# Loading the second table of the taps' transform behind the taps, four small edits early in the token stage, and later first one-hot bursts

## The chip, the cores and the metric

The kernel runs on one core of one Trainium2 chip. The metric is the device time of one execution in microseconds (us). Five engines work side by side, each through its own instructions in order: TensorE (PE in the profile; its weight loads are PEld), VectorE (DVE), ScalarE (ACT), GpSimd (POOL) and SyncE (SP), whose queue issues nearly all DMA transfers. They meet only at semaphores: an instruction whose input is not there yet holds up everything behind it on its own engine.

## The reference, cut to what matters

```python
x = A_u                                              # 2048 tokens x 576 channels
g = sigmoid((x * gate_w).sum(-1, keepdims=True))
# a: a long convolution along the tokens, each channel with its own 2048 taps
K = einsum("dn,dnl,dn->dl", C, exp(dt * A * l), dt * B).real
a = irfft(rfft(x, 4096) * rfft(K, 4096))[:2048] + x * Dskip
# b: experts chosen by product keys, 32 heads, 4096 experts
q = einsum("nd,dhc->nhc", x, w_q)
s1, s2 = q[..., :128] @ k1.T, q[..., 128:] @ k2.T    # 64 scores each; the best 2 of each
cand = the 4 sums of the best; the 2 largest go through a softmax -> gate, expert index
b = sum over heads and choices of gate * gelu(x . u[index]) * v[index]
out = g * a + (1 - g) * b
```

## The kernel before, in words

All matrix work runs on TensorE, most of it as three half-precision products per wanted product (a value is split into a high and a low f16 part: high x high, high x low, low x high). The stages, with the names that the profile shows for the tiles that TensorE writes:

- Start: the first 512 tokens (tile xs, its last 64 channels xr) and the first 512 experts' input rows (us, ur) are loaded in pieces; ScalarE squares each piece, small matmuls with a matrix of ones add the squares up (tile sq), VectorE makes power-of-two scales from the sum (`root_scale`), and both are split into f16 parts (xb and uhl; the part above 512 rows of the weights is wrem). For the first tokens six matmuls into a bank named x run ahead with results that nobody reads.
- Token stage: every token with every expert (tile a: 8 expert blocks of 512, 4 token blocks of 512, 4 matmul groups each) and the scores of the keys (tile s: 8 x 16 groups). A group is 14 matmuls of 512 columns. VectorE takes the best of the scores (MAX8, FIND_INDEX8); the results of a go as `go` to a buffer in memory, g_d. Between these groups stand 16 steps of the first Fourier stage of the tokens (`u_stage1`, tile u), the generation of the taps (phases kP, products on GpSimd and VectorE, then matmuls into tile kb, stored to k_d), and the folding of the keys into the query weights (wb).
- `freq()` starts when the last taps are on their way to k_d. It loads the tables of the taps' transform (tk, two of 1 MB) and the taps (ksb, four loads of 128 partitions x 9216 bytes from k_d), runs `k_stage1` (32 steps, tile k, step w reads table w // 16), then the frequency products (pr, pi, pv). `v_norm`, started by it, adds up the squares of the experts' output rows v; its one matmul (pvn) gives their scale, and only then `v_work` splits the eight tables vhl: table c is loaded into the place of table c + 1, the last one into a slot called vs; ScalarE writes each high part, VectorE the low part with SCALAR_TENSOR_TENSOR, two rows of blocks (a pair of instructions) at a time, two pairs per table.
- Last stage, one of 16 token tiles after the other in the order 0, 15, 1, 14, 2, ...: `prep(t)` loads g_d back (gl), applies the gelu on ScalarE, builds one-hot tiles A and Bg on VectorE (`onehot`, four sets, q = 0 to 3), multiplies them on TensorE into tile S (two sets to a burst, bursts named S1_0/S1_1 and S1_2/S1_3 for token tile 1), multiplies gl by S on VectorE, and splits the product into wh. Then 192 matmuls of 288 columns per token tile (tile o) multiply wh by the tables vhl in the order of the experts: 24 matmuls per table. `y_part` (tile y) adds the convolution's result.

The order of the instructions is set when the program is built. Generators yield to one another; each engine has a running estimate of when it will be free (class `Engine`, `dma`, `mm`), `ready` and `need` hold a piece of work until its inputs and its PSUM banks are estimated to be there, and `late` adds to that estimate. Whoever is ready first is written first, so a small change of one estimate can change the order of everything behind it. Nothing is decided at run time: what the estimate has wrong becomes a wait.

All matmuls come from the helper on line 214, all vector and scalar instructions from line 134, all DMA issues from line 205.

Of the kernel before, what the change touches and what calls it, by code (L numbers as in the profile page):

```python
# [18 lines left out]
OP = mybir.AluOpType  # L19
# [119 lines left out]
def body(ctx: ExitStack, tc: tile.TileContext, xT, au, par, logdt, dskip, gatew, wq, kT, uT, vv,  # L139
# [305 lines left out]
    def squares(a, r, sq, dst):  # L445

        acc = newcol(), newcol()
        S.activation(sq[:, 0:4, :], a, AF.Square, accum_out=sc[:, acc[0]])
        S.activation(sq[:, 4, :], r, AF.Square, accum_out=sc[:, acc[1]])
        yield from ready(sq)  # L450
        tag = side()
        yield from need(tag)
        p = bank(tag, "sq")
        mm(p[:, 0:2], onesb, short(acc[0].start, 2), True, True, 0.05)
        yield from ready(p)
        V.tensor_reduce(out=dst, in_=p[:, 0:2], axis=AX, op=OP.add)
        free(tag, dst)

    marks = {"x": [], "s": [], "h": [], "u": []}
    first_u = [None, None]  # L460
    ahead, normed = [], []

    def x_norm(tb, sq):

        yield from need("kb")
        p = bank("kb", f"x{tb}")
# [36 lines left out]
    def scale_first(a, r, sq, keep=None):  # L503
# [13 lines left out]
        p = bank("kb", "sq")  # L517
        for n, c in enumerate(acc):
            mm(p[:, 0:1], onesb, short(c.start, 1), n == 0, n == len(PARTS), 0.05)
# [554 lines left out]
    def u_stage1():  # L1074
# [32 lines left out]
        for p in range(NT):  # L1107
# [18 lines left out]
            for hh in range(2):  # L1126
                cs = slice(288 * hh, 288 * hh + 288)
                for n, (z, w) in enumerate(((0, 0), (0, 1), (1, 0))):
                    for g in range(2):
                        r = slice(64 * g, 64 * g + 64)  # L1130
                        mm(pbs[hh][g][:, :288], tu[r, z], h[r, w, cs], n == 0, n == 2, 0.063)
# [144 lines left out]
    def freq():  # L1276
# [7 lines left out]
        for w0, tkt in zip((0, 16), tabs):  # L1284
            dma(tkt, tk_d[:, w0:w0 + 16, :])
        for j in range(4):
            while wire[0] > clock[0] + 2:
                yield 0.3
            dma(ksb[:, j].rearrange("p c w i -> p c (w i)"),
                k_d[:, 32 * j:32 * j + 32].rearrange("c l z m n -> (l z m) c n"))  # L1290
        spawn(v_norm(), 12)
# [28 lines left out]
    def u_load(c):  # L1320
# [3 lines left out]
        if c:  # L1324
            dma(a, uT[0:512, cs].rearrange("(k p) n -> p k n", p=128))
        dma(r[0:64], uT[512:576, cs])
        if c:
            dma(r[64:128], uT[512:576, cs])
        else:
# [5 lines left out]
    def u_build(c):  # L1335
# [24 lines left out]
        if c == 0:  # L1360
            for k in range(4):
                S.activation(hl[:, 0, k, :], a[:, k, :], AF.Copy, scale=s)
# [147 lines left out]
    def prep(t):  # L1510
# [19 lines left out]
        for q in (0, 2):  # L1530
            yield from ready(*oh[q], *oh[q + 1], late=2.5 if t in ORDER[:3] else 0.0)
# [335 lines left out]
```

## Time and profile before

| what | value |
|---|---|
| median of 3 runs (lowest, highest) | 1441.61 us (1441.29, 1444.52) |
| profiled execution, its own time | 1442.26 us |
| span from the first to the last instruction in it | 1440.3 us |
| TensorE busy | 1421.2 us, 99% of the span |
| VectorE busy | 1161.8 us, 81% |
| ScalarE / GpSimd busy | 769.9 us / 484.2 us |
| granted TensorE clock | 1.000 |

The span leaves 19.1 us in which TensorE does nothing. An engine's idle time is given with what ended it: `[0.58 <-DMA ksb<-k_d]` means 0.58 us of idle time before this row, ended by the landing of that transfer. A timeline row is start, duration, engine, line, operation, out<-in, and xN where N like instructions were merged; the next start tells more than the duration, since matmuls and vector instructions overlap their ends.

### The profile page before, as it was taken

The numbers are of one execution on the slowest core, as the hardware profiler recorded it, in microseconds if no ns is written. First come the engines' busy times: TensorE is split into PE (matmuls) and PEld (weight loads), VectorE is DVE, ScalarE is ACT, GpSimd is POOL, SyncE is SP. The second block draws the span as 40 slices with busy tenths as digits, with TensorE's granted clock in tenths as the row PEclk, the third lists the DMA queues.
The fourth block names the chain that finished last, engine by engine and source line by source line (L and its number), as shares of the span: only waits on it lengthen the run. The fifth ranks groups of instructions, "written<-read, shape, count | busy, mean of one in ns | idle before, by whom it ended". The sixth has DMA issues, their size and how long they took to land.

```text
span 1440.3 us, 40769 instructions
## 1 busy us (share of the span) xinstructions
PE 1421.2 (99%) x16151; PEld 835.6 (58%) x16153; DVE 1161.8 (81%) x4595; ACT 769.9 (53%) x1281; POOL 484.2 (34%) x492
## 2 busy tenths in 40 slices
PE   7999999999999999999999999999999999999999
PEld 3444445455455445455555444456787787787785
DVE  6899899879886997875999897689877777877840
ACT  6346876796784876844655655666333223323310
POOL 0325357547356346230547899700000000000000
PEclk9999999999999999999999999999999999999999
DMA  8235323442334323159675677967443332442400
GB/s 302 75 116 165 90 74 121 126 144 72 109 100 154 93 93 115 49 172 308 222 264 191 243 258 271 307 216 249 151 131 130 117 122 95 136 147 69 159 10 17
DMA packets 134239, 215.43 MB, mean 150 GB/s; under 512 B 11040, under 2 KB 79904, under 8 KB 127648
## 3 DMA queue, kind: packets, MB, share of 16 engines
q1 hardware_dynamic: 133952, 212.80, 45.2%
q8 instruction: 127, 2.08, 0.6%
q14 instruction: 64, 0.52, 0.1%
q10 hardware_dynamic: 96, 0.02, 0.0%
HBM read 141.48 MB, written 71.30 MB: 148 GB/s over the span
## 4 chain that ended last, share of the span: by engine, by line
PE 87%; DVE 5%; DMA 1%; issue 0%; ACT 0%; SPq 0%; DVEq 0%
PE o L214 25%; PE s L214 24%; PE a L214 21%; PE S L214 3%; PE kb L214 2%; PE pr L214 2%; PE wb L214 2%; PE pv L214 1%; PE y L214 1%; PE kP L214 1%; PE k L214 1%; PE u L214 1%; DVE vhl L134 1%; DMA wq<-in_wq_dram 1%; DVE gl L134 1%; DVE A L134 1%
## 5 line engine op out<-in xcount | busy, mean ns | idle before, releaser
L214 PE MATMUL o<-vhl,wh 128*128 128x288 f16 (+2 forms) x3072 | 382.7, 286 | 0.0
L214 PE MATMUL s<-whl,xb 128*128 128x512 f16 x1536 | 363.9, 379 | 0.0
L214 PE MATMUL a<-xb,uhl 128*128 128x512 f16 x1536 | 358.8, 379 | 0.5 <-ACT uhl L134 0.3
L214 PEld LDWEIGHTS <-wh 128*128 128x128 f16 x3072 | 292.4, 98 | 84.1 <-issue 3.7
L214 PEld LDWEIGHTS <-xb 128*128 128x128 f16 x1792 | 170.7, 98 | 209.2 <-issue 14.5
L214 PEld LDWEIGHTS <-uhl 128*128 128x128 f16 x1536 | 147.3, 98 | 177.4 <-issue 3.2
L134 DVE FIND_INDEX8 i<-m,s 128x8 uint32<-128x64 f32 x1024 | 206.1, 219 | 0.0
L134 ACT ACTIVATE wh<-gl,s_wg 128x1024 f16<-128x1024 f32 x64 | 69.0, 1137 | 197.5 <-DVE gl L134 197.5
L134 DVE MAX8 m<-s 128x8 f32<-128x64 f32 x1024 | 145.9, 212 | 30.4 <-PE s L214 29.4
L134 POOL TENSOR_TENSOR CS<-CS,ex 128x512 f32<-128x512 f32 x72 | 98.0, 1392 | 147.5 <-DVE ex L134 146.1
L134 DVE TENSOR_TENSOR gl<-S,gl 128x256 f32<-128x256 f32 x256 | 88.4, 413 | 36.8 <-PE S L214 36.8
L134 ACT ACTIVATE go<-a,i_a 128x512 f32<-128x512 f32 x93 | 62.5, 684 | 97.2 <-PE a L214 70.2
L134 POOL TENSOR_TENSOR e<-aN,rt 128x512 f32<-128x512 f32 x72 | 83.2, 1176 | 49.9 <-PE kb L214 43.8
L134 DVE TENSOR_TENSOR A<-iota_a,vals 128x2048 f16<-128x2048 f16 x64 | 77.9, 1217 | 23.3 <-PE S L214 23.3
L134 ACT ACTIVATE gl<-gl 128x1024 f32<-128x1024 f32 x64 | 63.6, 1045 | 45.3 <-DMA gl<-g_d 36.8
L134 DVE SCALAR_TENSOR_TENSOR wh<-gl,s_wg,wh 128x1024 f16<-128x1024 f32 x62 | 77.6, 1279 | 12.4 <-ACT wh L134 12.3
L214 PE MATMUL s<-wrem,xb 128*128 128x512 f16 x256 | 76.2, 379 | 0.0
L214 PE MATMUL a<-xb,wrem 128*128 128x512 f16 x256 | 75.9, 379 | 0.0
L134 DVE MATCH_VALUE_LOAD i<-m,s 128x8 f32 x1024 | 69.4, 68 | 0.1
L134 ACT ACTIVATE CS<-CS 128x1024 f32<-128x1024 f32 x57 | 59.2, 1044 | 7.3 <-DVE CS L134 7.3
L134 POOL TENSOR_TENSOR ex<-ex,gN 128x512 f32<-128x512 f32 x36 | 44.8, 1256 | 53.3 <-ACT ex L134 53.1
L134 DVE SCALAR_TENSOR_TENSOR ya<-o,om,ya 128x288 f32<-128x288 f32 (+2 forms) x32 | 15.1, 512 | 55.4 <-PE o L214 55.4
(209 smaller groups left out, 2098.3 us busy)
## 6 DMA issues: line engine op xcount, KB each, us to landing
g_d<-go SPq DMA_DIRECT2D x128, 256.0 KB, 2.5
gl<-g_d SPq DMA_DIRECT2D x32, 1024.0 KB, 5.5
wq<-in_wq_dram SPq DMA_DIRECT2D x16, 1152.0 KB, 5.6
su_d<-us SPq DMA_DIRECT2D x32, 288.0 KB, 2.6
sk_d<-k1o SPq DMA_DIRECT2D x32, 288.0 KB, 2.7
ui<-su_d SPq DMA_DIRECT2D x16, 576.0 KB, 3.9
ki<-sk_d SPq DMA_DIRECT2D x16, 576.0 KB, 5.5
vn<-in_vv_dram SPq DMA_DIRECT2D x32, 288.0 KB, 5.4
```

The source lines that it names most:

```text
L134: return f(*a, **k)
L214: T.matmul(o, l, r, start=start, stop=stop)
```

## The change

Seven places of the source change. In `squares` the small square (the last channels) is now written ahead of the large one, and in `u_load` the small loads ahead of the large one for the expert blocks after the first. The bank x0 is taken early and nine more matmuls with unread results are spread over the two sums of squares at the start (`scale_first`). The first block of 512 columns of uhl is split between ScalarE and VectorE. In `u_stage1` the low table's product is moved ahead of the product with the low part of the input, so that this low part (tile uh, written last) is read by the last four of twelve matmuls and not by the third to sixth of a half. The second tk table is issued behind the four loads of the taps. The first three token tiles' one-hot bursts get 3.8 instead of 2.5 added to their estimate.

```diff
--- before.py
+++ after.py
@@ -445,8 +445,8 @@
     def squares(a, r, sq, dst):
 
         acc = newcol(), newcol()
+        S.activation(sq[:, 4, :], r, AF.Square, accum_out=sc[:, acc[1]])
         S.activation(sq[:, 0:4, :], a, AF.Square, accum_out=sc[:, acc[0]])
-        S.activation(sq[:, 4, :], r, AF.Square, accum_out=sc[:, acc[1]])
         yield from ready(sq)
         tag = side()
         yield from need(tag)
@@ -458,12 +458,14 @@
 
     marks = {"x": [], "s": [], "h": [], "u": []}
     first_u = [None, None]
+    first_x = []
     ahead, normed = [], []
 
     def x_norm(tb, sq):
 
-        yield from need("kb")
-        p = bank("kb", f"x{tb}")
+        if tb:
+            yield from need("kb")
+        p = bank("kb", f"x{tb}") if tb else first_x[1]
         if tb == 0:
             for k in range(6):
                 mm(p, onesb, sq[:, k % 4, :], True, True)
@@ -515,7 +517,14 @@
         yield from ready(sq)
         yield from need("kb")
         p = bank("kb", "sq")
+        if keep is None:
+            yield from need("kb")
+            first_x.extend((sq, bank("kb", "x0")))
+        idle_on, over = first_x
+        idle_at = ((), (4,) * 4, (0,), (2,)) if keep is None else ((), (), (0, 1), (2,))
         for n, c in enumerate(acc):
+            for k in idle_at[n]:
+                mm(over, onesb, idle_on[:, k], True, True)
             mm(p[:, 0:1], onesb, short(c.start, 1), n == 0, n == len(PARTS), 0.05)
         yield from ready(p)
         out = root_scale(p[:, 0:1], 1.02)
@@ -1123,9 +1132,9 @@
             yield from need(tag, 4)
             hungry[0] = False
             pbs = [[bank(tag, f"u1_{p}_{g}_{hh}") for g in range(2)] for hh in range(2)]
-            for hh in range(2):
-                cs = slice(288 * hh, 288 * hh + 288)
-                for n, (z, w) in enumerate(((0, 0), (0, 1), (1, 0))):
+            for n, (z, w) in enumerate(((0, 0), (1, 0), (0, 1))):
+                for hh in range(2):
+                    cs = slice(288 * hh, 288 * hh + 288)
                     for g in range(2):
                         r = slice(64 * g, 64 * g + 64)
                         mm(pbs[hh][g][:, :288], tu[r, z], h[r, w, cs], n == 0, n == 2, 0.063)
@@ -1281,13 +1290,13 @@
         ksb = KS.__enter__().tile([128, 4, NCK // 2, 32, 2 * NI], F16, name="ksb")
         fk = FK.__enter__()
         tabs = [fk.tile([128, 16, 2, 128], F16, tag="tk", name=f"tk{w0}", bufs=2) for w0 in (0, 16)]
-        for w0, tkt in zip((0, 16), tabs):
-            dma(tkt, tk_d[:, w0:w0 + 16, :])
+        dma(tabs[0], tk_d[:, 0:16, :])
         for j in range(4):
             while wire[0] > clock[0] + 2:
                 yield 0.3
             dma(ksb[:, j].rearrange("p c w i -> p c (w i)"),
                 k_d[:, 32 * j:32 * j + 32].rearrange("c l z m n -> (l z m) c n"))
+        dma(tabs[1], tk_d[:, 16:32, :])
         spawn(v_norm(), 12)
         spawn(gating(0), 20)
         yield from k_stage1(ksb, fk, tabs)
@@ -1321,11 +1330,10 @@
         a = slot([4, 512], F32, f"us{c}")
         r = actp.tile([128, 512], F32, tag="ur", name=f"ur{c}")
         cs = slice(512 * c, 512 * c + 512)
-        if c:
-            dma(a, uT[0:512, cs].rearrange("(k p) n -> p k n", p=128))
         dma(r[0:64], uT[512:576, cs])
         if c:
             dma(r[64:128], uT[512:576, cs])
+            dma(a, uT[0:512, cs].rearrange("(k p) n -> p k n", p=128))
         else:
             halves_load(a, uT, cs)
         return a, r
@@ -1359,7 +1367,10 @@
         rem = wrems[c % 2]
         if c == 0:
             for k in range(4):
-                S.activation(hl[:, 0, k, :], a[:, k, :], AF.Copy, scale=s)
+                w = 512 if k else 256
+                S.activation(hl[:, 0, k, :w], a[:, k, :w], AF.Copy, scale=s)
+                if k == 0:
+                    V.tensor_scalar(hl[:, 0, k, w:], a[:, k, w:], s, None, op0=OP.mult)
                 marks["h"].append(S.free + 0.28)
             S.activation(rem[:, 0, :], r, AF.Copy, scale=s)
             marks["h"].append(S.free + 0.28)
@@ -1528,7 +1539,7 @@
                 yield 0.3
             oh = {q: onehot(t, q) for q in range(3)}
         for q in (0, 2):
-            yield from ready(*oh[q], *oh[q + 1], late=2.5 if t in ORDER[:3] else 0.0)
+            yield from ready(*oh[q], *oh[q + 1], late=3.8 if t in ORDER[:3] else 0.0)
             yield from need("wb", 4)
             pbs = []
             for d in (q, q + 1):
```

Up to the 25th step of the phases (near 465 us of the trace before) TensorE's order is the same but for the nine added matmuls and the exchange in u. From there on the order differs until the third pair of token tiles of the last stage, and is the same again to the end. Three places of it follow. Names end in the buffer's number, which differs between the two programs.

SyncE's queue where the transform's tables (tk0, tk16) and the taps (ksb) are loaded, before:

```order
L205 DMA wq5_0_8158<-in_wq_dram 128x2304
L205 DMA tk0_8173<-in_tk_dram 128x4096
L205 DMA tk16_8174<-in_tk_dram 128x4096
L205 DMA ksb_8169<-k_d_68 128x18x256
L205 DMA g_d_65<-go6_0_1_8295 128x4x128
L205 DMA ksb_8169<-k_d_68 128x18x256
L205 DMA wq5_1_8348<-in_wq_dram 128x2304
L205 DMA g_d_65<-go6_0_2_8359 128x4x128
L205 DMA g_d_65<-go6_0_3_8385 128x4x128
L205 DMA ksb_8169<-k_d_68 128x18x256
L205 DMA g_d_65<-go6_1_0_8405 128x4x128
L205 DMA ksb_8169<-k_d_68 128x18x256
```

and now:

```order
L205 DMA wq5_0_8056<-in_wq_dram 128x2304
L205 DMA k_d_68<-ko_8207 128x1024
L205 DMA tk0_8267<-in_tk_dram 128x4096
L205 DMA ksb_8263<-k_d_68 128x18x256
L205 DMA wq5_1_8315<-in_wq_dram 128x2304
L205 DMA ksb_8263<-k_d_68 128x18x256 x3
L205 DMA tk16_8268<-in_tk_dram 128x4096
L205 DMA g_d_65<-go6_1_1_8433 128x4x128
```

The loads of the taps stand closer together with one load of query weights (wq) between them, and the second table behind them. On TensorE, counted in the order, 170 matmuls of 512 columns stood between the last taps' products (kb34) and the first step of k before; 104 stand there now, and the two foldings wb5 in both.

SyncE's queue at the last two loads of the v tables, vhl7 (raw rows of table 6) and vs (of table 7), before:

```order
L205 DMA vhl7_12507<-in_vv_dram 128x4x576
L205 DMA g_d_65<-go7_1_0_13173 128x4x128
L205 DMA g_d_65<-go7_1_1_13201 128x4x128
L205 DMA g_d_65<-go7_1_2_13220 128x4x128
L205 DMA vs_13408<-in_vv_dram 128x4x576
L205 DMA g_d_65<-go7_1_3_13418 128x4x128
L205 DMA g_d_65<-go7_2_0_13423 128x4x128
L205 DMA g_d_65<-go7_2_1_13436 128x4x128
L205 DMA g_d_65<-go7_2_2_13591 128x4x128
L205 DMA gl1_0_13616<-g_d_65 128x2048
L205 DMA gl1_1_13617<-g_d_65 128x2048
```

and now:

```order
L205 DMA vhl7_12509<-in_vv_dram 128x4x576
L205 DMA gl1_0_13608<-g_d_65 128x2048
L205 DMA gl1_1_13609<-g_d_65 128x2048
L205 DMA g_d_65<-go7_2_3_13633 128x4x128
L205 DMA db_13658<-in_dskip_dram 128x576
L205 DMA tf0_13663<-in_tf_dram 128x256
L205 DMA yz0_13662<-z_d_69 128x1x576 x4
L205 DMA ya0_13660<-in_au_dram 32x576 x4
L205 DMA ya15_13661<-in_au_dram 32x576 x4
L205 DMA vs_13890<-in_vv_dram 128x4x576
```

The load of vs stood ahead of gl1, the gelu input of token tile 1; it now stands behind gl1 and behind the inputs of y. The matmul pvn, from which the v tables' scale comes, stood 316 matmuls of a ahead of the first o before and stands 266 ahead of it now.

VectorE's queue after the last one-hot set of token tile 1 (Bg1_3), before, where the last pair for table 7 comes behind four products with S:

```order
L134 TENSOR_TENSOR Bg1_3_13865<-Be1_3_13863,vals_80 128x512 x2
L134 TENSOR_TENSOR gl1_0_13616<-S1_0_0_13729,gl1_0_13616 128x16x16
L134 TENSOR_TENSOR gl1_1_13617<-S1_0_0_13729,gl1_1_13617 128x16x16
L134 TENSOR_TENSOR gl1_0_13616<-S1_0_1_13730,gl1_0_13616 128x16x16
L134 TENSOR_TENSOR gl1_1_13617<-S1_0_1_13730,gl1_1_13617 128x16x16
L134 SCALAR_TENSOR_TENSOR vhl7_12507<-vs_13408,sci_76,vhl7_12507 128x576 x2
L134 TENSOR_TENSOR gl1_0_13616<-S1_1_0_13795,gl1_0_13616 128x16x16
```

and now, some twenty rows further on, from the last products of S1_3 to the second pair for table 7:

```order
L134 TENSOR_TENSOR gl1_1_13609<-S1_3_0_14024,gl1_1_13609 128x16x16
L134 TENSOR_TENSOR gl1_0_13608<-S1_3_1_14025,gl1_0_13608 128x16x16
L134 TENSOR_TENSOR gl1_1_13609<-S1_3_1_14025,gl1_1_13609 128x16x16
L134 SCALAR_TENSOR_TENSOR ya0_13660<-y0_0_0_14143,iuk_94,ya0_13660 128x288
L134 SCALAR_TENSOR_TENSOR ya0_13660<-y0_0_1_14148,iuk_94,ya0_13660 128x288
L134 SCALAR_TENSOR_TENSOR wh1_1_14109<-gl1_0_13608,s_wg_92,wh1_0_14108 128x1024
L134 SCALAR_TENSOR_TENSOR vhl7_12509<-vs_13890,sci_76,vhl7_12509 128x576 x2
L134 SCALAR_TENSOR_TENSOR ya15_13661<-y0_1_0_14153,iuk_94,ya15_13661 128x288
L134 SCALAR_TENSOR_TENSOR ya15_13661<-y0_1_1_14158,iuk_94,ya15_13661 128x288
L134 SCALAR_TENSOR_TENSOR wh1_1_14109<-gl1_0_13608,s_wg_92,wh1_0_14108 128x1024
L134 SCALAR_TENSOR_TENSOR vhl7_12509<-vs_13890,sci_76,vhl7_12509 128x576 x2
```

Between Bg1_3 and the second pair for vhl7 VectorE had the four products of S1_0 and that pair itself before. Now it has: the products of S1_0, one wh15, the second pair of vhl5, the products of S1_1, the first pair of vhl6, the products of S1_2, the two products of ya with Dskip, the second pair of vhl6, and the rows shown. TensorE's matmuls of o0 stand around the bursts of token tile 1 as 42, 72, 36, y, 42 before and as 48, 72, 36, y, 36 now; the matmuls on vhl5b, vhl6 and vhl7 each carry a wait for VectorE now, and carried none for it before.

## The prediction

> **What bounds the kernel now.** The page's first part and the waits of TensorE come first.
>
> ```profile
> PE 1421.2 (99%) x16151; PEld 835.6 (58%) x16153; DVE 1161.8 (81%) x4595; ACT 769.9 (53%) x1281; POOL 484.2 (34%) x492
> PE u L214 <- DVE uh L134: 2.0, 2, 1.4
> PE sq L214 <- ACT uhl L134: 1.4, 2, 1.0
> PE S L214 <- DVE gl L134: 0.7, 2, 0.5
> PE k L214 <- DMA ksb<-k_d: 0.6, 1, 0.6
> ```
>
> TensorE sets the end: 1421.2 us of a span of 1440.3. Work that other engines do costs nothing until TensorE meets an input that is not there. The change adds nine matmuls in gaps and otherwise no TensorE work, so its worth lies in these waits and in new ones. The waits it aims at are small: two of u, one sq, two of S and one of k, 4.7 us, and 0.35 us of idle time at the start. Since TensorE is hardly ever late, the place where another engine is nearly late matters more than the average. A table by stretches shows it, around the second u and in the last stage before and during the first token tile (columns: stretch, its length, then busy time and count of PE, PEld, DVE, ACT and POOL, the granted clock, the DMA share and GB/s):
>
> ```profile
> 97.00:117.00 20.00, 18.58 (x95) 8.38 (x96) 19.82 (x110) 7.51 (x15) 11.83 (x9) 1.00 0.42 139
> 947.00:961.00 14.00, 14.00 (x322) 8.15 (x319) 10.77 (x23) 7.19 (x12) 0.00 (x0) 1.00 0.65 200
> 961.00:991.00 30.00, 30.00 (x379) 15.07 (x378) 29.86 (x51) 20.43 (x26) 2.23 (x1) 1.00 0.79 259
> 991.00:1007.30 16.30, 16.30 (x276) 13.06 (x275) 16.13 (x28) 12.44 (x14) 2.56 (x1) 1.00 0.74 246
> ```
>
> The first row has TensorE idle for 1.4 us while VectorE works all the time. In the last stage VectorE has 3.2 us to spare up to 961, and from 961 to 1007.3 us it has no idle time worth naming (29.86 of 30.00, 16.13 of 16.30), while TensorE runs without a gap. Whatever is moved into this stretch of VectorE's queue comes out later by its own length.
>
> **The start.** The added matmuls lie in idle time. What counts is when the first a starts.
>
> ```profile
> 9.25 2.72 PE L214 MATMUL x<-xb,onesb 128*128 128x512 bf16 x6
> 12.63 1.24 PE L214 MATMUL x<-xb,onesb 128*128 128x512 bf16 x5
> 13.44 2.56 ACT L134 ACTIVATE uhl<-us,sci 128x512 f16<-128x512 f32 x4 [0.89 <-DVE sci L134]
> 14.21 2.76 PE L214 MATMUL a<-xb,uhl 128*128 128x512 f16 x12 [0.35 <-ACT uhl L134]
> 16.51 0.29 ACT L134 ACTIVATE vals<-kt 128x128 bf16<-128x128 f32 x1
> 16.86 0.22 PE L214 MATMUL kn<-vals,onesb 128*128 128x128 bf16 x1
> ```
>
> The first uhl piece takes 2.56/4 = 0.64 us on ScalarE. Halved, it takes about 0.4, with no more on VectorE beside it, which makes the xb pieces later by as much; the third of them is read sixteen matmuls after the first. At most the idle 0.35 us before a goes. kn, twelve matmuls later, then waits for ScalarE's vals, which ends only 0.06 us before it now, so some 0.1 us comes back: gain 0.2. The six early matmuls run at 2.72/6 = 0.45 us each, the five at 12.63 at half that, so the array sped up between them. If it is still slow when the new ones are queued ahead of the last sq, three of them at 0.45 against a gap of that order push sq back by up to 0.4 us. I take 0.1 us of gain, ends -0.3 and +0.2. [...]
>
> **Squares, loads and u.**
>
> ```profile
> 79.18 1.91 ACT L134 ACTIVATE uhl<-us 128x2048 bf16<-128x2048 f32 x1 [2.11 <-DMA us<-in_uT_dram]
> 81.85 0.16 PE L214 MATMUL sq<-sc,onesb 128*128 128x2 bf16 x1 [0.95 <-ACT uhl L134]
> 115.48 1.41 DVE L134 SCALAR_TENSOR_TENSOR uh<-us,sci,uh 128x576 f16<-128x576 f32 x1
> 116.94 0.79 PE L214 MATMUL u<-uh,tu 64*128 64x288 f16 x10 [1.42 <-DVE uh L134]
> ```
>
> With the small pieces first, the large square is the last to run and waits for the last load. The 0.8 us of the small square leave the path, up to 0.9 us are added for two small loads (256 KB at about 300 GB/s) ahead of the large one: sq moves by -0.8 to +0.4. Either way the end is not moved: VectorE is busy 19.82 of 20 us up to 117 and releases u at 115.48 + 1.41. In the new order eight of twelve matmuls of u (four pairs) run ahead of that wait instead of two (one pair), so only 2/12 instead of 5/6 of 0.79 - 0.06 us remain behind it: about 0.4 us gained, once, since the earlier wait of u ends in the same VectorE backlog. Ends 0 and 0.7.
>
> **The taps' tables.**
>
> ```profile
> 636.35 0.29 PE L214 MATMUL kb<-e,CS 128*32 128x64 f32 x8
> k_d<-ko SPq DMA_DIRECT2D x18, 256.0 KB, 2.4
> 643.38 0.82 SPq L205 DMA_DIRECT2D tk<-in_tk_dram  x2
> 679.11 1.14 PE L214 MATMUL k<-ksb,tk 128*128 128x288 f16 x8 [0.58 <-DMA ksb<-k_d]
> 690.82 2.25 PE wb L214 x72
> 644.00:654.00 10.00, 10.00 (x48) 4.56 (x47) 9.86 (x79) 4.00 (x7) 0.00 (x0) 1.00 0.97 357
> 658.00:664.00 6.00, 6.00 (x90) 3.87 (x91) 3.44 (x11) 3.03 (x8) 0.00 (x0) 1.00 1.00 296
> ```
>
> Moving 1.05 MB behind the taps frees about 3 us of transfer time at 357 GB/s. But the planner has moved the first k closer: 104 matmuls and two foldings after the last kb, 104 x 0.22 (from 14.21 to 16.86 for twelve) + 2 x 2.25 = 27.4 us, where 170 stood before. The first table was issued 6.7 us after the last kb (636.64 to 643.38), behind VectorE's work on ko and the store of 2.4 us; with VectorE less behind it may be 4.5. Then come tk0, four ksb of 1.18 MB and one wq of 1.18 MB: 6.95 MB at 357 to 296 GB/s, 19.5 to 23.5 us, and 1.5 us until the last one is told of (the 2.4 us of a 256 KB store, less 0.9 at 296 GB/s): 25.5 to 31.7 us. The wait at k is 0 to 4.3 us instead of 0.58. I take 1.1, 0.5 more, since the loads now stand together in SP's queue. tk16 is not needed before step 16, far behind.
>
> **The one-hot bursts and what follows them.** The later estimate moves S1_2 six matmuls on, 0.7 us, about the two waits of S above. But the planner's new order also brings the v tables later, and these rows price it:
>
> ```profile
> 991.02 5.31 PE L214 MATMUL o<-vhl,wh 128*128 128x288 f16 x42
> 992.10 1.21 DVE L134 TENSOR_TENSOR A<-iota_a,vals 128x2048 f16<-128x2048 f16 x1
> 1000.08 3.42 DVE L134 SCALAR_TENSOR_TENSOR vhl<-vs,sci,vhl 128x576 f16<-128x576 f32 x2
> 1007.29 1.41 DVE L134 TENSOR_TENSOR gl<-S,gl 128x256 f32<-128x256 f32 x4
> 1008.62 1.53 DVE L134 SCALAR_TENSOR_TENSOR vhl<-vs,sci,vhl 128x576 f16<-128x576 f32 x2
> 1010.08 1.41 DVE L134 TENSOR_TENSOR gl<-S,gl 128x256 f32<-128x256 f32 x4
> 1011.40 1.27 DVE L134 SCALAR_TENSOR_TENSOR wh<-gl,s_wg,wh 128x1024 f16<-128x1024 f32 x1
> 1013.92 1.41 DVE L134 TENSOR_TENSOR ya<-ya,db 128x576 f32<-128x576 f32 x2
> 1016.25 15.61 PE L214 MATMUL o<-vhl,wh 128*128 128x288 f16 x126
> 1016.43 2.19 ACT L134 ACTIVATE wh<-gl,s_wg 128x1024 f16<-128x1024 f32 x2 [12.08 <-DVE gl L134]
> 1016.59 0.93 DVE L134 SCALAR_TENSOR_TENSOR ya<-y,iuk,ya 128x288 f32<-128x288 f32 x2
> ```
>
> Before, VectorE ends the last pair of vhl7 at 1010.08. o0 reads that pair in its last twelve matmuls; o0 ends 42 x 15.61/126 = 5.2 us after 1016.25, at 1021.5, so the pair is 10 us early. Now take D = the end of Bg1_3, 1007.29 before. From D VectorE's queue holds, up to the second pair of vhl7, four groups of four products with S (1007.29 to 1008.62, 1.33 each), five pairs for vhl (1008.62 to 1010.08, 1.46 each), three wh (to 1.2 each), the product with Dskip (1.3) and two ya from y (0.9 each): 5.3 + 7.3 + 3.6 + 1.3 + 1.8 = 19.3 us, where 2.8 stood before. ScalarE's high parts for wh1 come only after the last gl (1.1 each), with the table's behind them: 0.7 more. Then twelve matmuls, 1.5 us. o0 ends at D + 21.5; before, 1021.5 - 1007.29 = 14.2. D itself: S15's last burst now ends five matmuls (1.1 us) ahead of o0 instead of eleven, so VectorE's list from 992.10 to 1007.29, of the same kinds, starts about 1.1 us later against o0. Together 7.3 + 1.1 = 8.4 us. The pair at 1000.08 took 3.42 instead of 1.53; if that collision falls outside the list now, 1.9 less.
>
> A second way to it goes by pvn, which starts the tables:
>
> ```profile
> L214 PE MATMUL pvn<-nut,onesb x1: 177/177/177, 903.5 to 903.5; 128*128 128x1 bf16 x1
> 906.04 0.38 PE L214 MATMUL pr<-ui,cst 64*64 64x192 f32 x2
> 907.52 2.12 PE L214 MATMUL a<-xb,uhl 128*128 128x512 f16 x9
> ```
>
> It stood 87.5 us ahead of o0 (903.5 to 991.02). Now 50 matmuls of a fewer lie between them, 11 us, and three frequency products with their pv as well (one of them takes from 906.04 to 907.52, 1.5 us: 4.5 for three): it stands 15.5 us closer. With the same pace from pvn to the last pair, that pair ends 1010.08 - 991.02 + 15.5 = 34.6 us into o0, and o0 ends 36.1 us after its start, where it took 30.5: 5.6 more. The two ways give 8.4 (6.5 without the collision) and 5.6. I take 7.5, nearer the first, because there the queue's order is known row by row; ends 3 (VectorE saving its 3.2 us of spare time before 961, and half a collision) and 10.3 (a second collision).
>
> **The sum.** 7.5 + 0.5 - 0.1 - 0.4 = 7.5 us (the S waits are inside the first term). The profiled execution becomes 1442.26 + 7.5 = 1449.8, its span 1447.8; the median, 0.65 lower, 1441.61 + 7.5 = 1449.1. I say 1449.
>
> **Rivals.** (1) No new wait at o0: VectorE reaches D with eight microseconds in hand, because it has more idle time than I think ahead of 961 us and ends the early pairs there. It decides from a last pair of vhl7 that ends within 29 us of o0's start. For it: VectorE's 3.2 us of spare time before 961. Against it: the order puts five pairs behind Bg1_3, whose set TensorE's burst of S1_3 itself needs. Then S's 0.7 goes too: 1441.6 - 0.7 - 0.4 - 0.1 + 0.5 = 1440.9, not slower; up to 1444 with a partial wait. (2) The taps come late as well: 4.3 us at k instead of the 1.1 that I take, on top of o0: 1449.1 + 3.2 = 1452.3. For it, the lower rate of 296 GB/s; against it, no store of go stands between the loads any more. (3) The change does what it aims at and nothing else: every named wait goes with the idle time before a, 5 us: 1436.6. Against it, the changed order of the middle of the kernel.
>
> **How the numbers follow.** Forecast 0.70, own range 1446 to 1452; rival 1 0.20; rival 2 0.07; rival 3 0.03. About 0.3% (4.3 us) is what a measurement of this kernel can tell from no change. Faster by more: rival 3, 0.03. Within: rival 1, 0.20. Slower: the forecast and rival 2, 0.77. The range 1443 to 1453.5 leaves out the lower half of rival 1 and rival 3.
>
> **What would show it.** Right: in the waits of TensorE new rows of o for VectorE's or ScalarE's vhl, 6 to 9 us together, near o0's last 36 matmuls, o0 taking 37 to 40 us from its first matmul to its last instead of 30.5, and the S wait at token tile 1 unchanged or gone; one u wait near 1.0; k's wait between 0 and 2. Wrong: no wait of o above 2 us, or a time below 1446; then the step with D failed. A loss at k or in the token stage instead would make the time right for a wrong reason.

## The result and the profile after

The changed kernel takes 1456.34 us (median; 1453.82 to 1457.21) against 1443.43 us of the kernel before in the same runs: ratio 1.0089, 95% interval 1.0079 to 1.0100, so 12.9 us slower. The profiled execution has a span of 1454.4 us, 14.1 more than before. All ratios here are of fast executions; one execution of e13 below, 2087 us at a granted clock of 0.655 beside 1441 to 1446 us for its nine others, is left out as slow. The page's first line and the longest waits of TensorE, but for those of sq, all ahead of the second u (us in total, times, longest):

```profile
PE 1427.2 (98%) x16159; PEld 836.1 (57%) x16162; DVE 1173.9 (81%) x4611; ACT 764.6 (53%) x1270; POOL 476.1 (33%) x488
PE wn L214 <- ACT wj L134: 3.8, 4, 1.8
PE o L214 <- DVE vhl L134: 2.4, 4, 1.0
PE o L214 <- ACT vhl L134: 2.2, 1, 2.2
PE k L214 <- DMA ksb<-k_d: 2.0, 1, 2.0
PE a L214 <- DVE i L134: 1.5, 1, 1.5
PE k L214 <- DVE i L134: 1.1, 1, 1.1
PE u L214 <- DVE uh L134: 1.1, 1, 1.1
PE S L214 <- DVE gl L134: 1.1, 2, 0.6
```

The waits of o for vhl that the prediction named are there. Those of wn (small matmuls that add up ScalarE's squares wj of the query weights), of a, and of k on a bank (the last two end with VectorE's i) are not in it at all. One wait of before has gone; "issue" means that TensorE waited for nothing that the profile shows:

```profile
PE kb L214 <- issue: 1.5, 1, 1.5
```

Where the 14.1 us lie, by the start of the same matmul in both traces:

| from | to | before, us | after, us | more |
|---|---|---|---|---|
| start of the span | first kb | 163.99 | 163.77 | -0.2 |
| first kb | first o | 827.03 | 833.81 | 6.8 |
| first o | last o of the first token tile | 30.26 | 37.64 | 7.4 |
| there | last matmul | 415.54 | 415.68 | 0.1 |

The second row is nearly the sum of its waits: 3.8 + 2.0 + 1.5 + 1.1 = 8.4 against 1.5 + 0.6 before, 6.3 more. The third row is the predicted place. VectorE's timeline in it (start, duration, ..., the idle time before in brackets):

```profile
1014.43 0.76 DVE L134 TENSOR_TENSOR Bg<-Be,vals 128x512 f16<-128x512 f16 x2
1015.11 1.41 DVE L134 TENSOR_TENSOR gl<-S,gl 128x256 f32<-128x256 f32 x4
...
1023.20 1.42 DVE L134 TENSOR_TENSOR ya<-ya,db 128x576 f32<-128x576 f32 x2
...
1028.41 1.29 DVE L134 SCALAR_TENSOR_TENSOR wh<-gl,s_wg,wh 128x1024 f16<-128x1024 f32 x1 [0.16 <-ACT wh L134]
1029.62 1.54 DVE L134 SCALAR_TENSOR_TENSOR vhl<-vs,sci,vhl 128x576 f16<-128x576 f32 x2
...
1033.25 1.54 DVE L134 SCALAR_TENSOR_TENSOR vhl<-vs,sci,vhl 128x576 f16<-128x576 f32 x2
```

Bg1_3 ends at 1015.19, the last pair of vhl7 at 1034.79: 19.6 us, where 2.8 us stood before. TensorE waits for it, and runs at half its clock for a while (0.50 granted from 1030.17 to 1033.58 us). TensorE's timeline, and the table by stretches (granted clock in the third column from the end):

```profile
1025.40 1.39 PE L214 MATMUL o<-vhl,wh 128*128 128x288 f16 x10 [0.30 <-DVE vhl L134]
1029.03 0.41 PE L214 MATMUL o<-vhl,wh 128*128 128x288 f16 x2 [2.25 <-ACT vhl L134]
1030.48 3.04 PE L214 MATMUL o<-vhl,wh 128*128 128x288 f16 x12 [1.05 <-DVE vhl L134]
1034.12 1.75 PE L214 MATMUL o<-vhl,wh 128*128 128x288 f16 x13 [0.59 <-DVE vhl L134]
```

```profile
1029.00:1030.00 1.00, 0.41 (x2) 0.19 (x2) 1.00 (x2) 1.00 (x2) 0.00 (x0) 1.00 0.93 350
1030.00:1034.00 4.00, 3.04 (x12) 1.77 (x12) 3.96 (x7) 4.00 (x6) 0.00 (x0) 0.57 0.56 168
1034.00:1035.00 1.00, 0.88 (x8) 0.71 (x8) 1.00 (x3) 1.00 (x2) 0.00 (x0) 1.00 0.73 156
```

The slow clock costs nothing here: after those twelve matmuls TensorE is early once more and waits 0.59 us for the last pair. The waits of o for vhl are 4.6 us together. The rest of the 7.4 us is these twelve matmuls (3.04 us instead of the 1.5 us that the prediction has for twelve), 0.3 us more of waits of S, and what is lost at each stop and start.

### The profile page after: what moved, and what is told of

Same layout as the page of the kernel before. It is cut to its first block, busy times and chain, and to the rows that moved or that the text cites. A ratio compares the mean times of both kernels' runs of the same rounds, so it can differ in the third digit from the quotient of the medians.

```text
span 1454.4 us, 40799 instructions
## 1 busy us (share of the span) xinstructions
PE 1427.2 (98%) x16159; PEld 836.1 (57%) x16162; DVE 1173.9 (81%) x4611; ACT 764.6 (53%) x1270; POOL 476.1 (33%) x488
## 4 chain that ended last, share of the span: by engine, by line
PE 84%; DVE 5%; DMA 3%; SPq 1%; ACT 1%; issue 1%; POOL 0%; ACTq 0%; DVEq 0%
PE o L214 25%; PE a L214 22%; PE s L214 21%; PE S L214 3%; PE kb L214 2%; PE pr L214 2%; PE wb L214 2%; PE pv L214 1%; PE kP L214 1%; SPq L205 1%; DVE i L134 1%; PE y L214 1%; PE k L214 1%; PE u L214 1%; DMA ksb<-k_d 1%; DMA wq<-in_wq_dram 1%
## 5 line engine op out<-in xcount | busy, mean ns | idle before, releaser
L134 ACT ACTIVATE go<-a,i_a 128x512 f32<-128x512 f32 x86 | 58.3, 684 | 93.1 <-PE a L214 68.3
```

What stands on the lines that cost most here:

```text
L134: return f(*a, **k)
```

## The experiments

### Which of the edits it is

Two kernels have one edit alone, two have all but one:

```diff
# e1: before + only this          e3: the changed kernel without it
+            for n, (z, w) in enumerate(((0, 0), (1, 0), (0, 1))):
+                for hh in range(2):
...
# e2: before + only this          e4: the changed kernel without it
+        dma(tabs[0], tk_d[:, 0:16, :])
...
+        dma(tabs[1], tk_d[:, 16:32, :])
```

> The kernel before with the new order of the u matmuls alone (first hh inside, the low part of uh read last). Theory 'queue': o0 is as long as VectorE's queue behind the one-hot set Bg1_3 makes it. Here that queue holds 11.1 us of work up to the last pair of vhl7 (19.9 in the changed kernel, 2.9 before), Bg1_3 ends about 17.6 us into o0, so the last pair is there 28.7 us into o0, o0 needs it after 29: o0 30.3 to 32 us instead of 37.6. Rival 'u carries all': the order of the u matmuls alone gives the whole loss, o0 37 to 38 us and 1455 to 1457 us in all. On the 6.6 us that are lost ahead of o0: if they come from the u order, the first o starts at 995 to 998 us; if they come from the second table's place, at 990 to 992. Time by 'queue' with the loss ahead of o0 from the second table: 1441 to 1444; with it from the u order: 1447 to 1450.

> The kernel before with the second table's load behind the taps alone. Theory 'queue': the last pair of vhl7 now stands 15.8 us of VectorE work ahead of Bg1_3, so o0 stays at 30.3 us. The last wq load stands behind the loads ui1 and ki1 of the frequency products, as in the changed kernel: if the waits of wn there (3.8 us) come from that, they are back here, the first o starts at 993 to 995 us and the time is 1444 to 1447. Rival: the waits ahead of o0 come from the u order, and the first o starts at 989 to 992 us, time 1440 to 1443. Rival 'second table carries all': 1455 to 1457.

> The changed kernel with the old order of the u matmuls, all six other edits kept. Theory 'queue': the last pair of vhl7 is 2.5 us of work ahead of Bg1_3, o0 30.3 us. The last wq load stands behind ui2 and ki2 here. If the second table's place makes the waits of wn, 3 to 4 us of them stay and the time is 1444 to 1447; if the u order makes them, the time is 1440 to 1443. If neither edit matters alone (the loss is of the other five), 1450 or more.

> The changed kernel with the second table's load back ahead of the taps, all six other edits kept. Theory 'queue': 11.1 us of work from Bg1_3 to the last pair of vhl7, o0 30.3 to 32 us. The last wq load stands ahead of ui0: no wait of wn if the second table's place makes it. Then 1441 to 1444; if the waits ahead of o0 come from the u order, 1447 to 1450.

| kernel | ratio to before (95%) | first o at, us | o0, us | Bg1_3 to last pair of vhl7, us |
|---|---|---|---|---|
| before | 1 | 991.0 | 30.3 | 2.8 |
| changed | 1.0089 (1.0079 to 1.0100) | 997.6 | 37.6 | 19.6 |
| e1, u order alone | 1.0097 (1.0080 to 1.0114) | 1006.2 | 33.0 | 10.9 |
| e2, second table alone | 1.0009 (0.9999 to 1.0018) | 994.7 | 29.2 | -15.8 |
| e3, all but the u order | 1.0001 (0.9991 to 1.0010) | 989.2 | 31.8 | -2.3 |
| e4, all but the second table | 1.0082 (1.0065 to 1.0099) | 1004.8 | 29.4 | 10.9 |

The loss goes with the u order, with or without the six other edits, and the second table's place, after which the change is named, is worth about nothing in time (e2: +0.1%, not told from none). But the loss does not sit in one place: in e1 and e4 nearly all of it comes ahead of the first o, in the changed kernel half of it lies in o0. The waits of e1:

```profile
PE a L214 <- DVE vals L134: 3.8, 1, 3.8
PE tr L214 <- ACT go L134: 2.9, 1, 2.9
PE wn L214 <- ACT wj L134: 2.2, 3, 1.1
PE o L214 <- issue: 2.0, 1, 2.0
```

(tr are products with an identity matrix, which transpose the chosen places.) As far as waits for vhl go, the theory of VectorE's queue holds over six kernels: with the last pair 10.9 us behind Bg1_3 or nearer, no wait for vhl is left in o0, with 19.6 us there are 4.6 us of them. The length of o0 it gives less well. The 33.0 us of e1 (30.3 to 32 expected) hold 2.0 us in which o waits for nothing that the profile shows and 3.4 us at half the clock. In e3 the negative number doesn't mean an early table: Bg1_3 itself ends 33.6 us into o0, the last pair 31.4 us, just in time, and 2.2 us of waits of y and o for other inputs make o0 31.8 instead of 30.3 us.

"u carries all" is right in the total and wrong in the place. The times of e1 and e4, 1457.4 and 1455.4 us, are 5 to 7 us above the 1447 to 1450 that "queue" gave them, because the first o comes at 1006.2 and 1004.8 us and not at 995 to 998. The waits of wn follow neither edit alone: they are 2.2 us in e1 and e2, 3.7 in e4 and none in e3, so the expectations that tied them to the second table's place missed.

### What the chip does, and what the planner does

The new order of the twelve u matmuls does two things. On the chip it reads the low part last. (In the old order the third and fourth matmul of each half read it; the fifth and sixth only stand behind them.) In the program's estimate (`mm` notes a bank as ready 0.4 us after its last matmul) it makes the first two u banks ready four matmuls later, 4 x 0.063 = 0.25 us (the 0.31 us in an expectation below is a slip). The two can be had apart: e5 has the new order, with the old times noted; e6 has the old order, with the new times noted.

```diff
# e5: the changed kernel, behind the u matmuls
+            for g in range(2):
+                rdy[key(pbs[0][g])] = clock[0] - (7 - g) * 0.063 + 0.4
# e6: the kernel before, behind the u matmuls
+            for g in range(2):
+                rdy[key(pbs[0][g])] = clock[0] - (3 - g) * 0.063 + 0.4
```

> The changed kernel, whole, but the planner is told that the two first u banks are complete when they were in the old order (0.25 us and 0.31 us earlier than the new order makes them). So the chip runs the new order of the u matmuls, and everything else comes in the order of the kernel without that edit. Theory 'planner': the loss of 13 us is the planner's answer to those 0.3 us, and nothing that the twelve matmuls do on the chip; here 1441.5 to 1444, with no wait of o over 1 us. Rival 'chip': reading the low part last, or closing all four banks together, itself delays what follows: 1453 to 1458.

> The kernel before with its own order of the u matmuls on the chip, but the planner is told that the first two u banks are complete 0.25 us later, as in the new order. Theory 'planner': the same instruction order elsewhere as with the new u order alone, so the same loss, 1454 to 1459, and waits of tr and a near 940 us again. Rival 'chip': 1441 to 1445.

e5: ratio 0.9989 (0.9980 to 0.9999), o0 31.8 us. e6: 1.0113 (1.0091 to 1.0135), 1460.9 us and so a little more than expected, first o at 1006.7 us, with waits of 3.0 us of tr at 942.5 us and 3.4 us of a at 946.8 us. The loss follows the note and not the matmuls. With all seven edits in, e5 has none of the long waits (those of sq, all ahead of the second u, are left out again):

```profile
PE u L214 <- DVE uh L134: 1.1, 1, 1.1
PE k L214 <- DVE i L134: 1.1, 1, 1.1
PE y L214 <- ACT wh L134: 1.0, 1, 1.0
PE o L214 <- issue: 0.4, 1, 0.4
```

### How little it takes

If the planner answers to the note, how large must it be? Writing the program with other shifts gives the orders without a run: 0.02 us at all sixteen u steps leaves every instruction where it was; 0.05, 0.1, 0.15, 0.2, 0.25, 0.3 and 0.4 us all give one and the same other order, that of e1. Of the sixteen steps only the eleventh gives this order. What tips there is one line of the taps' generation, which picks the engine for the absolute value of a block of phases:

```
        if S.free <= V.free:        # ScalarE reckoned free no later than VectorE
            ...
            S.activation(v[:, 0:2], v[:, 2:4], AF.Abs)
        else:
            V.tensor_scalar(...)
```

In the kernel before VectorE has it, for the 26th block (CS25):

```profile
465.70 0.69 DVE L134 TENSOR_SCALAR CS<-CS 128x1024 uint32<-128x1024 uint32 x1
```

e12 tells the planner 0.05 us at the eleventh step and changes nothing else. e13 moves just this instruction to ScalarE and tells the planner nothing, so that all others keep their places.

```diff
# e12: the kernel before, behind the u matmuls
+            if p == 10:
+                for g in range(2):
+                    rdy[key(pbs[0][g])] += 0.05
# e13: the kernel before, in the else branch above (VectorE's instruction is noted, but not written)
...
+            if c == 25:
+                nc.scalar.activation(v[:, 0:2], v[:, 2:4], AF.Abs)
```

> The kernel before, with one number changed: at one of the sixteen u steps, the eleventh, the planner is told that the first two u banks are complete 0.05 us later. No matmul is moved by hand. Theory 'planner': one choice tips (the absolute value of a block of phases goes to ScalarE instead of VectorE, since ScalarE is now reckoned free first), the rest of the order comes out as with the new u order alone, and so does the time: 1454 to 1461. Rival: a shift this small costs what it says, 1441 to 1445.

> The kernel before with exactly one instruction moved: the absolute value of the 26th block of phases (VectorE, 0.69 us at 465.70) is done by ScalarE, where the tipped choice puts it, and the planner is not told, so that every other instruction of every engine keeps its place. Theory 'cascade': the moved instruction costs nothing, what costs is that the planner writes all later work in another order: 1441 to 1445, first o at 990 to 993 us. Rival 'the instruction itself': ScalarE is later by about 1 us at the taps and that shift grows: 1447 or more.

e12: ratio 1.0114 (1.0098 to 1.0130), 17 us, for a note of 0.05 us. e13: 1.0004 (0.9994 to 1.0015), first o at 992.7 us. The instruction itself costs nothing; the order that the planner writes once it stands elsewhere costs everything. In e12 TensorE waits twice near 944 us as in e1 (2.95 us of tr, 3.13 us of a), and its clock is halved for 10 us from 943.3 us on:

```profile
943.00:948.00 5.00, 0.98 (x16) 0.89 (x16) 0.52 (x4) 3.85 (x8) 0.00 (x0) 0.53 0.77 269
948.00:953.00 5.00, 4.87 (x12) 1.78 (x12) 4.93 (x12) 0.00 (x0) 0.00 (x0) 0.50 0.01 2
```

Did the planner see it coming? Its own clock, printed while it writes the program, beside the chip's (its zero is not quite the span's; the margin is the first less the second):

| kernel | first o, planner | chip | margin | last matmul, planner | chip |
|---|---|---|---|---|---|
| before | 1007.4 | 991.0 | 16.4 | 1460.3 | 1436.8 |
| changed | 1004.5 | 997.6 | 6.9 | 1464.5 | 1450.9 |
| e1 | 1004.2 | 1006.2 | -2.0 | 1457.0 | 1454.7 |
| e2 | 1005.2 | 994.7 | 10.5 | 1458.1 | 1440.4 |
| e5 | 1007.4 | 990.1 | 17.3 | 1461.2 | 1439.4 |

In its own clock the other order reaches the first o 3 us earlier, with less reserve, and the chip does not follow. The 7.4 us of waiting inside o0 of the changed kernel are in the plan (it waits 1.6 and 5.8 us there); the losses ahead of the first o are not.

### The wait at o0 by itself

In the changed kernel every instruction keeps its place; only VectorE's six on y for the first two token tiles are left out (e9: these tiles lack the convolution's part) or run twice (e10: their result is changed by it).

```diff
# e9 with n = 0, e10 with n = 2: an instruction is reckoned once and written n times
+                V.times = n if p == 0 else 1
                 V.tensor_mul(a, a, db)
+                V.times = 1
...
+                    V.times = n if p == 0 else 1
                     V.scalar_tensor_tensor(ah, pbs[2 * n + hh][:, :288], iuk, ah, op0=OP.mult, op1=OP.add)
+                    V.times = 1
```

> The changed kernel, every instruction in the same place, but VectorE's six instructions on y for the first pair of token tiles (two products with Dskip, four sums) are left out, so that the convolution's part of these two tiles is missing. They stand between Bg1_3 and the last pair of vhl7 and take 1.33 + 0.93 + 0.94 = 3.2 us. Theory 'queue': VectorE's list behind Bg1_3 sets when o0 ends, so o0 shrinks from 37.6 to 34.4 to 35.2 us and the time by 2.4 to 3.2 us, ratio to before 1.0067 to 1.0073 instead of 1.0089. Rival 'table load': the last table's load, which lands at 1024 us behind the y loads in SP's queue, or ScalarE's high parts behind it set the end, and o0 stays at 37 to 38 us.

> The changed kernel with the same six VectorE instructions run twice (the result of the two token tiles changes by it). Theory 'queue': o0 grows from 37.6 to 40.4 to 41.2 us, the time by 2.8 to 3.4 us, ratio to before 1.0108 to 1.0115. Rival 'table load': o0 37 to 38.5 us, ratio 1.0085 to 1.0095.

| | Bg1_3 to last pair, us | o0, us | ratio to before |
|---|---|---|---|
| e9, left out | 18.3 | 36.4 | 1.0085 (1.0071 to 1.0100) |
| changed | 19.6 | 37.6 | 1.0089 (1.0079 to 1.0100) |
| e10, twice | 23.0 | 42.1 | 1.0109 (1.0094 to 1.0125) |

Longer work behind Bg1_3 comes out in full: 3.4 us of it, 4.4 us in o0, of which 1.0 us comes behind the last pair, at half the clock (1031.2 to 1041.4 us). Less work does not: of 3.2 us left out only 1.3 are won. VectorE of e9 shows why (its line numbers are one further):

```profile
1025.98 1.41 DVE L135 TENSOR_TENSOR gl<-S,gl 128x256 f32<-128x256 f32 x4
1028.40 1.28 DVE L135 SCALAR_TENSOR_TENSOR wh<-gl,s_wg,wh 128x1024 f16<-128x1024 f32 x1 [1.01 <-ACT wh L135]
...
1032.04 1.29 DVE L135 SCALAR_TENSOR_TENSOR wh<-gl,s_wg,wh 128x1024 f16<-128x1024 f32 x1 [0.89 <-ACT wh L135]
1033.24 1.54 DVE L135 SCALAR_TENSOR_TENSOR vhl<-vs,sci,vhl 128x576 f16<-128x576 f32 x2
```

ScalarE's high parts for wh1 are 1.9 us behind VectorE's queue and take its place. So "queue" is right for the changed kernel, with ScalarE close behind it; the table's load, which landed at 1024 us in the changed kernel, is not what o0 waits for. The ratio of e9 doesn't show the 1.2 us: in the profiled execution its clock was halved once more, at 782 us (1.7 us lost).

### Whether the two losses add

e11 takes ScalarE's squares of the last eighth of the query weights out of the changed kernel, which wn waits for (its scale comes from the wrong eighth).

```diff
+        S.times = 0 if c == 7 else 1
         for n in range(2):
             S.activation(fl(junk), fl(w[:, 2 * n:2 * n + 2]), AF.Square, accum_out=sc[:, acc[n]])
+        S.times = 1
+        sums[c, h] = sums[6, h] if c == 7 else acc
...
```

> The changed kernel, every instruction in the same place, but ScalarE's four squares of the last eighth of the query weights are left out, and wn reads the sums of the eighth before (the scale of the last eighth comes from the wrong part of the weights). So wn at 764 to 782 us has no ScalarE work to wait for: the 3.4 us of waits there go. Theory 'sum': the waits ahead of o0 and the wait at o0 add up, the first o starts 3 to 3.6 us earlier, o0 stays at 37.6 us, ratio to before 1.0064 to 1.0070. Rival 'cover': VectorE's backlog runs on its own time, the first o starts earlier but o0 grows by the same 3 us, and the ratio stays at 1.0085 to 1.0092.

The waits of wn at 764 to 782 us are gone. From the first kb to the first o there are 831.6 us instead of 833.8: 2.2 us won of the 3.4, since the frequency products and the s groups behind wait 1.0 us instead. The last pair of vhl7 ends 37.21 us after the first o, as in the changed kernel (37.21): VectorE moves with TensorE, the two losses add and don't cover each other. The ratio, 1.0074 (1.0060 to 1.0088), lies between the two forecasts and doesn't tell them apart. The profiled execution, the slowest of five, is no shorter than the changed kernel's (1454.4 us both): it has half the clock for 13.7 us in three places (6.8 us lost, 1.7 in the changed kernel), its first kb comes 0.6 us later, and o0 ends 1.0 us later after the first o (38.6 us), behind the last pair and at half the clock.

### The small edits

e7 has the four edits that leave the order of the token stage alone (the order of the small loads in `u_load` is not among them and was run only together with others); e8 adds the new u order with the old times noted. e14 has only the nine extra matmuls (and the bank x0 taken early), e15 the small square first and the split first piece of uhl without them.

```diff
# e7 = these hunks of the change: squares, x_norm and scale_first, u_build, prep
# e8 = e7 +
+            for n, (z, w) in enumerate(((0, 0), (1, 0), (0, 1))):
...
+                rdy[key(pbs[0][g])] = clock[0] - (7 - g) * 0.063 + 0.4
# e14 = x_norm and scale_first          e15 = squares and u_build
```

> The kernel before with those edits that leave TensorE's order from the generation of the taps to the first token tile as it was: the small square first, the extra matmuls at the start, the split first piece of uhl, the later one-hot bursts. They act on 0.35 us ahead of the first a, on 1 us ahead of sq and on 0.7 us at S: between -1.5 and +0.5 us, 1441.5 to 1443.5 beside a kernel before of 1443.0; not told from no change.

> The same four edits and the new order of the u matmuls, with the planner told the old times of the two banks. The second wait of u shortens by 0.4 us (0.2 to 0.7) against the run before it; everything else is the same order: 0 to -1 us beside it, 1441 to 1443 beside a kernel before of 1443.0.

> The kernel before with the nine extra matmuls at the start alone (and the bank x0 taken early). In all nine profiles of kernels that have them with the other edits of the start, the first twelve matmuls of a took 2.6 us; in four of five without them 3.3 to 4.1 us. Theory 'warm': the extra matmuls alone do it, kn comes 2.6 us after the first a, kb starts at 163 to 165 us. Rival 'other edits' (the split first piece of uhl): 3.3 us or more between a and kn. The time is 0 to -1.5 us beside the kernel before; not told from no change.

> The kernel before with the small square first and the split first piece of uhl, without the extra matmuls. Theory 'warm': the first twelve matmuls of a are slow again, 3.3 to 4.1 us to kn (with a chance of about one in five of 2.6). Rival 'other edits': 2.6 us. Time between -0.5 and +0.5 us beside the kernel before.

e7 0.9999 (0.9990 to 1.0008), e8 0.9991 (0.9981 to 1.0001), e14 1.0014 (1.0005 to 1.0024), e15 1.0001 (0.9990 to 1.0012): none is 0.2% away from 1, and e14, for which 0 to -1.5 us was expected, is rather slower, by 2 us. Its profile has no stretch at half clock and an o0 of 30.3 us, but one wait that no other has: 1.56 us of a at 32.13 us for ScalarE's go. There, too, the order is another one: ScalarE has two of the first three results of a, behind its squares of the query weights, where VectorE had two before. That this is the 2 us was not tested. From e7 to e8 the wait of u falls from 1.42 to 1.05 us, and the first kb starts at 163.45 and 163.43 us: nothing is left of it, since the sum of squares ahead waits 0.4 us longer. The best kernel is e5 (ratio 0.9989) with e8 beside it, 1 to 2 us better than before if at all: the interval of e5 ends at 0.9999, that of e8 at 1.0001.

What the extra matmuls do is seen at the first twelve matmuls of a, here in e14 and (without them) e13:

```profile
14.80 2.75 PE L214 MATMUL a<-xb,uhl 128*128 128x512 f16 x12
17.39 0.22 PE L214 MATMUL kn<-vals,onesb 128*128 128x128 bf16 x1
```

```profile
14.83 3.68 PE L214 MATMUL a<-xb,uhl 128*128 128x512 f16 x12
18.35 0.22 PE L214 MATMUL kn<-vals,onesb 128*128 128x128 bf16 x1
```

From the first a to kn: 2.59 to 2.65 us in all ten profiles with the extra matmuls, 3.26 to 4.25 us in six of seven without. The seventh is the kernel before's own, 2.64 us. "Warm" holds: e15 has 4.25 us. (The views give a granted clock of 1.00 there for all of them, but the traces of the kernel before and of the changed kernel have no clock record ahead of 12.4 and 13.0 us, where the record of the full clock begins, in both ahead of the first a at 14.21 and 14.63 us.) In the time nothing of it is seen: the first kb of e14 comes at 165.94 us, that of e13 at 165.51.

## Why the prediction was right or wrong, point by point

The direction was right, and its largest term as well; the time, 1449 us with 1443 to 1453.5, was 7.3 us short of the measured 1456.34; 1.8 us of that lie in the kernel before, which took 1443.43 us beside it and not 1441.61. By its steps:

- **D and what stands behind it** (19.3 us from Bg1_3 to the last pair of vhl7; Bg1_3 16.3 + 1.1 us into o0; the sum 7.5 us at o0, o0 of 37 to 40 us). Measured 19.6, 17.6, 7.4 and 37.6 us. Right in the mechanism, VectorE's queue, and in its length. The waits of o for vhl are 4.6 us, less than the 6 to 9 named as a sign, because TensorE spent part of the time at half the clock instead of waiting (3.04 us for the twelve matmuls from 1030.48 us). The pair of vhl that takes 3.42 us came again, at 1007.89, inside the list ahead of Bg1_3; both times GpSimd's product for wh ran beside it (2.56 us from 999.60, 2.49 us from 1007.48), but that it is the cause was not tested.
- **The taps** (0.5 us more at k, 1.1 in all; "between 0 and 2"). The wait for ksb is 2.0 us, 0.9 more than taken, within the ends that the part gave. A second wait at k, 1.1 us for a bank that VectorE's i frees, was not in it.
- **The sum** is the step that failed. Apart from k it has no term for the token stage from the second u to its end, although the prediction said that the planner orders all of this anew. There wn (3.8), a (1.5) and the bank of k (1.1) wait, and the kb wait of 1.5 us goes: 4.9 us. With the 0.9 us at ksb that is 5.8 of the 6.6 us by which the span, forecast as 1447.8, was missed. The order was read at the places where a wait was expected, and the rest counted as unchanged.
- **The cause.** The later tables were put down to the planner's new order, without saying which edit makes it. e1 to e6 show that it is the u order's note to the planner, and not the second table, after which the change is named; so the part on the u matmuls (0.4 us gained) left out what that edit mostly does.
- **The start** (0.1 us gained, ends -0.3 and +0.2). Against the profile of before, kn comes 0.42 us later. But that profile was the quickest of seven without the extra matmuls; against their mean (kn at 18.4 us, 16.9 with them) it is 1.5 us earlier. The step took one execution's head for the kernel's. In the total nothing of it shows (e7, e14).
- **Squares, loads, u, S.** Hidden as said: sq waits 1.5 instead of 0.95 us, u starts in the same VectorE backlog. One wait of u of 1.1 us is left, 0.4 less than the second one before, as forecast (the 2/12 in the working is a slip for 4/12, with which its 0.4 us comes out). The S waits did not go: 1.1 instead of 0.7 us.
- **The rivals.** No new wait at o0: refuted. The taps late by 4.3 us: 2.0, so refuted. All named waits gone: refuted. The range missed because all its cases put the loss at o0 or at k; a loss in the token stage was named, but only as a way to be right for a wrong reason, and had no price.

## What to carry to other kernels

Where a program decides its order by comparing estimates, ask of every edit which notes it changes and which comparisons are close; a note moved by 0.25 us, or by 0.05, bought another order from the middle of this kernel on, at 13 to 17 us, where the edit itself was worth 0.4. To keep the edit and not the new order, hold the old note (e5). When the order changes, walk all of it engine by engine, not only the places where waits stood, and compare the head of a kernel over several profiles before crediting it to one.

## What the runs showed of the hardware

**TensorE ran at half the clock behind some waits, and the length of the waits alone does not tell behind which.** In e2 it did so behind two waits of 1.1 us within 2.4 us:

```profile
757.48 0.16 PE L214 MATMUL wn<-sc,onesb 128*128 128x1 bf16 x1 [1.10 <-ACT wj L134]
758.77 0.16 PE L214 MATMUL wn<-sc,onesb 128*128 128x1 bf16 x1 [1.13 <-ACT wj L134]
759.32 3.87 PE L214 MATMUL wb<-kt,wq 128*64 128x64 f32 x72
```

```profile
759.00:760.00 1.00, 1.00 (x20) 0.69 (x20) 0.90 (x7) 0.76 (x4) 0.84 (x4) 0.82 0.97 387
760.00:763.00 3.00, 3.00 (x60) 2.99 (x57) 2.46 (x23) 0.23 (x1) 0.83 (x3) 0.50 1.06 316
763.00:764.00 1.00, 1.00 (x9) 0.42 (x6) 0.00 (x0) 0.74 (x3) 0.00 (x0) 0.97 1.05 406
```

0.18 + 3 x 0.50 + 0.03 = 1.71 us of TensorE's time lost, and the 72 matmuls of wb take 3.87 us, where they took 2.25 before. Counted in stretches of half a microsecond from 20 us to the last matmul, the lost time is 0 in the kernel before, e3, e5, e7, e8, e13, e14 and e15; 1.7 us in the changed kernel and e2; 3.4 in e6 and e9; 5.1 in e4 and e12; 6.8 in e1, e10 and e11. At its own last waits of wn, near 782 us, the changed kernel has longer ones than e2, 1.77 and 1.12 us, and the clock stays at 1.00:

```profile
780.94 0.16 PE L214 MATMUL wn<-sc,onesb 128*128 128x1 bf16 x1 [1.77 <-ACT wj L134]
782.23 0.16 PE L214 MATMUL wn<-sc,onesb 128*128 128x1 bf16 x1 [1.12 <-ACT wj L134]
782.30:786.00 3.70, 3.70 (x46) 1.80 (x46) 3.36 (x12) 2.60 (x6) 3.62 (x5) 1.00 0.44 124
```

e9 is the same kernel up to there, and its clock is halved at this place:

```profile
782.60:785.80 3.20, 3.20 (x36) 1.47 (x28) 2.57 (x8) 1.52 (x3) 3.12 (x3) 0.50 0.66 178
```

What decides was not shown. In e2 the 1.71 us came on top of the 2.2 us of waiting; in o0 of the changed kernel, where the last pair of vhl7 was later still, the slow stretch cost nothing.
